# The head of the first expert's list in three pieces, and six more half chunks as split products whose low halves VectorE makes

## The chip, the core and the metric

The kernel runs on one core of a Trainium2 chip. Its time is the device time of one execution in microseconds (us). The engines work side by side, each on its own queue of instructions in order: TensorE (PE in the profile) multiplies, VectorE (DVE) and ScalarE (ACT) work on elements, GpSimd (POOL) issues gathers, scatters and accumulating transfers, SyncE (SP) issues most of the loads. Semaphores tie the queues together.

## The reference

Two parts follow each other. The first is an attention over channels: batch 4, 5056 positions, 256 channels.

```
qn = q / (norm(q, axis=1) + 1e-06);  kn = k / (norm(k, axis=1) + 1e-06)
s = kn.transpose(0, 2, 1) @ qn / tau          # 256 x 256 per batch
a = softmax(s, axis=-1)
x = v @ a                                     # 5056 x 256 per batch
```

The second is a mixture of eight experts over the 20224 rows of x. All 161792 logits are sorted; in that order each row goes to the first expert that still has room, with room for 2528 rows in each.

```
logits = x @ w_gate                           # 20224 x 8
for idx in argsort(-logits.flatten()):
    tok, e = idx // 8, idx % 8
    if assigned[tok] >= 0 or counts[e] >= 2528: continue
    assigned[tok] = e; counts[e] += 1
out[mask_e] = relu(x[mask_e] @ w1[e]) @ w2[e] # 256 -> 1024 -> 256
```

All of it is fp32, and the lists must come out as the sort makes them.

## The kernel before, in words

**Stages.** The scores k'q of the four batches come first, up to about 190 us, with the values of batch 0 among them. From 190 to 219 us stand the last softmax, the gates (a times w_gate) and the last logits. From 219 to 314 us stand the *turns*: the values of batches 1 to 3 that are still missing, and beside them the search for the first expert's list. Then the eight experts follow, layer 1 (line 1502) and layer 2 (line 1549), with the rows of each gathered from x_d in DRAM; the lists of the later experts are searched for beside these.

**Chunks and half chunks.** The 5056 rows of a batch are five chunks of eight tiles of 128 rows (the last is shorter). A half chunk is four tiles. Its x rows need eight products of 256 columns into two PSUM banks, which ScalarE empties (lines 271 and 587) and stores (line 277).

**Two kinds of products.** A plain half chunk (F in `TURNS`) multiplies in fp32 (line 267). A split one (C, "cloven") writes v and a as sums of a high part in the fp32r format and a low part, and adds three fp32r products: high by high, high by low, low by high (line 583). `PLAIN` and `CLOVEN` say which chunks are which: 16 half chunks F, of which 12 stand in the turns and four behind them, and 10 C. The split of v is `cleave`: ScalarE writes the negated v into the low tile (line 568), an accumulating transfer that GpSimd issues adds v once the copy is rounded, and ScalarE copies the high part (line 571). a of batch 2 is split by lines 550, 554 and 555 (`halve_a`). `PLACES` gives the tiles into which half chunks are split, and `BEHIND` the turn before which a tile is not free.

**The search.** The head of a list takes the largest logit of each row and its expert, and turns it into an integer key: two halves of 16 bits, `hi` and `klo`, and the expert's one-hot row `oh` (lines 611 to 660, 160 columns of 128 rows). The threshold is then found in eight rounds. In each, VectorE compares the keys with 15 thresholds (`ge`, line 730, in two halves), TensorE counts (20 products into one bank, line 695), VectorE takes sums of the counts (`Dm`, `Dr`, `Ex`, lines 698 to 704), TensorE totals them (line 708), and VectorE finds the hit and the next thresholds (`mxs`, `hit`, `thr`, lines 715 to 751). The lists are made from the threshold, and the rows gathered.

**Order.** From the turns on the program is written by a planner `o`. `o.tick` counts TensorE's time; a stream of steps (`yield ve(...)`, `yield "P", ...`) is given its place between the products by due times worked out from assumed costs, `o.post` places a single job, `FIRST_LAT` says from when VectorE is taken to be free for the first list. Each engine then works through its queue in that order.

Of the kernel before, what the change touches and what calls it, by code (L numbers as in the profile page):

```python
# [107 lines left out]
def attention_moe(ctx: ExitStack, tc: tile.TileContext, q, k, vt, tau, wg, w1t, w2t, tabs, out):  # L108
# [497 lines left out]

    def largest(to, x, tmp, n):
        while n > 1:
            h = n // 2
            yield ve(h * COLS)  # L610
            V.tensor_tensor(to[:, None] if n == 2 else tmp[:, 0:h], x[:, 0:h], x[:, n - h:n], op=OP.max)
            if n % 2:
                yield ve(COLS)
                V.tensor_tensor(to if n == 3 else tmp[:, 0], tmp[:, 0], x[:, h], op=OP.max)
            x, n = tmp, h

    def route(p, R):
# [10 lines left out]
        else:  # L628
            m = rtile("m")
            eq = rtile("eq", (128, E, COLS), BF)  # L630
            yield from largest(m, L, eq.bitcast(F32).rearrange("p r c -> p (r c)").rearrange("p (r c) -> p r c", c=COLS), R)
            key = rtile("t1").bitcast(I32)
            yield ve(COLS, 2)
            V.tensor_scalar(key.bitcast(F32), m, 0.0, None, op0=OP.add)
            flip = rtile("tie").bitcast(I32)
            yield ve(COLS, 2)
            V.tensor_scalar(flip, key, 31, 0x7fffffff, op0=OP.arith_shift_right, op1=OP.bitwise_and)
            yield ve(COLS)
            V.tensor_tensor(key, key, flip, op=OP.bitwise_xor)
            khi = rtile("khi", dt=I32)  # L640
            yield ve(COLS, 2)
            V.tensor_scalar(khi, key, -65536, None, op0=OP.bitwise_and)
            hi = rtile("hi", dt=I16)
            yield ve(COLS, 2)
            V.tensor_scalar(hi, khi, 1.0 / 65536.0, None, op0=OP.mult)
            klo = rtile("klo", dt=I32)
            yield ve(COLS, 2)
            V.tensor_scalar(klo, key, 0xffff, None, op0=OP.bitwise_and)
            yield ve(R * COLS)
            V.tensor_tensor(eq[:, 0:R], L[:, 0:R], m[:, None, :].to_broadcast([128, R, COLS]), op=OP.is_equal)  # L650
            yield ve(R * COLS)
            V.tensor_tensor(eq[:, 0:R], eq[:, 0:R], code9[:, 0:R, None].to_broadcast([128, R, COLS]), op=OP.mult)
            f = rtile("f")
            yield from largest(f, eq, eq, R)
# [1167 lines left out]
```

## Time and profile before

| what | us |
|---|---|
| median of three runs | 1213.45 |
| lowest and highest of them | 1211.61, 1217.76 |
| the profiled execution | 1215.57 |
| its span (first to last instruction) | 1213.8 |
| start of the turns in it | 219.13 |
| first product of layer 1 in it | 314.47 |

The profile is of one execution, and all rows below are of it. The span leaves out what lies around the first and the last instruction. A row of the timeline gives the start, the duration, the engine, the line, the operation, the tiles written and read, and in brackets how long the engine was idle before and what ended it. A product in fp32 has two records.

### The profile page before, as it was taken

What the parts mean: (1) busy time and instruction counts of PE and PEld (TensorE: products, weight loads), DVE (VectorE), ACT (ScalarE), POOL (GpSimd) and SP (SyncE); (2) the same over time, 40 slices, a digit from 0 to 9 for tenths busy, and PEclk for the clock granted to TensorE, in tenths of its full rate; (3) what the DMA queues carried; (4) which work ended last, traced back from release to release, by engine and by line L of the source; (5) the groups of instructions that cost most, each with busy time, mean ns of one, the idle gap of its engine ahead of it and who ended that gap; (6) DMA issues with size and microseconds to landing.
All of it is one profiled execution on the core that took longest, in us unless ns stands there. A gap on an engine that the chain in (4) does not pass through costs nothing.

```text
span 1213.8 us, 21117 instructions
## 1 busy us (share of the span) xinstructions
PE 1188.6 (98%) x7569; PEld 1044.0 (86%) x7569; DVE 891.1 (73%) x2493; ACT 597.7 (49%) x1314; POOL 453.1 (37%) x691
## 2 busy tenths in 40 slices
PE   7999999999999999999999999999999999999997
PEld 6889977898888888888888889888988898898997
DVE  6788695778788888988878788798786565555441
ACT  5667644655344444444454454464355644344331
POOL 1000001111353664555554554464444445444422
PEclk9999999999999999999999999999999999999999
DMA  8999996885335324534643454353234233433311
GB/s 304 356 397 318 409 321 213 181 235 218 108 101 151 88 72 128 167 92 116 172 127 88 107 165 140 100 156 121 86 124 145 86 119 124 145 94 99 108 61 35
DMA packets 76025, 193.50 MB, mean 159 GB/s; under 512 B 11792, under 2 KB 35600, under 8 KB 71312
## 3 DMA queue, kind: packets, MB, share of 16 engines
q0 software_dynamic: 26864, 74.08, 23.0%
q1 hardware_dynamic: 39088, 96.49, 22.8%
q10 hardware_dynamic: 9968, 21.59, 4.7%
q8 instruction: 59, 0.97, 0.3%
q14 instruction: 46, 0.38, 0.1%
HBM read 122.51 MB, written 58.98 MB: 150 GB/s over the span
## 4 chain that ended last, share of the span: by engine, by line
PE 80%; DVE 7%; issue 5%; DMA 3%; POOL 2%; ACT 2%; another core or an unknown queue 0%; SPq 0%; POOLq 0%; DVEq 0%; ACTq 0%
PE ph L1502 29%; PE py L1549 28%; PE s L345 8%; PE px L267 5%; PE pc L695 2%; PE px L308 2%; PE px L583 2%; DMA ua<-in_q_dram 2%; PE px L461 1%; POOL out_dram L1559 1%; DVE hL L1511 1%; DMA via<-xs 1%; DVE ua L1269 1%; PE pi L935 1%; DVE acc_k L355 1%
## 5 line engine op out<-in xcount | busy, mean ns | idle before, releaser
L1549 PE MATMUL py<-ua,hH 128*128 128x512 f32 (+2 forms) x1288 | 422.9, 382 | 0.0
L1502 PE MATMUL ph<-xH,ua 128*128 128x512 f32 (+1 forms) x1280 | 391.8, 380 | 0.8 <-DVE hL L1511 0.6
L1549 PE MATMUL py<-ua,hL 128*128 128x256 f32 (+1 forms) x1280 | 326.9, 275 | 0.0
L1506 ACT ACTIVATE hH<-ph 128x512 fp32r<-128x512 f32 (+1 forms) x320 | 189.3, 592 | 198.8 <-PE ph L1502 171.6
L1502 PEld LDWEIGHTS ph<-xH,ua 128*128 128x128 f32 x1280 | 241.1, 189 | 32.8 <-DVE hL L1511 4.2
L1511 DVE SCALAR_TENSOR_TENSOR hL<-ph,hH 128x512 fp32r<-128x512 f32 (+1 forms) x320 | 216.3, 677 | 62.4 <-ACT hH L1506 46.3
L1549 PEld LDWEIGHTS py<-ua,hH 128*128 128x128 f32 (+1 forms) x1288 | 233.0, 188 | 25.8
L1549 PEld LDWEIGHTS py<-ua,hL 128*128 128x128 f32 (+1 forms) x1280 | 242.4, 190 | 8.2
L1559 POOL DMA_INDIRECT out_dram<-y,idx x160 | 167.1, 1045 | 205.8 <-DVE y L1590 118.0
L1502 PE MATMUL ph<-xL,ua 128*128 128x512 f32 (+1 forms) x640 | 242.8, 379 | 0.7 <-DVE hL L1511 0.7
L1288 POOL DMA_INDIRECT xg<-x_d,src x160 | 163.7, 1023 | 80.1 <-issue 46.2
L345 PE MATMUL s<-ua 128*128 128x256 f32 (+1 forms) x640 | 144.0, 384 | 7.1 <-DMA ua<-in_q_dram 7.1
L345 PEld LDWEIGHTS s<-ua 128*128 128x128 f32 (+1 forms) x640 | 121.2, 192 | 26.5 <-DMA ua<-in_q_dram 7.5
L1502 PEld LDWEIGHTS ph<-xL,ua 128*128 128x128 f32 x640 | 121.0, 189 | 15.2 <-DVE hL L1511 1.1
L1570 ACT ACTIVATE y<-py 128x512 f32<-128x512 f32 x80 | 47.8, 597 | 114.9 <-PE py L1549 84.1
L1590 DVE TENSOR_TENSOR y<-py,y 128x256 f32<-128x256 f32 x79 | 33.5, 423 | 94.5 <-ACT y L1586 91.6
L354 ACT ACTIVATE sq<-ua 128x1024 f32<-128x1024 f32 (+1 forms) x80 | 76.6, 971 | 49.9 <-DMA ua<-in_k_dram 18.9
L1586 ACT ACTIVATE y<-py 128x256 f32<-128x256 f32 x80 | 30.6, 383 | 124.3 <-PE py L1549 106.4
L1299 POOL COPY spacer<-hH 1x1 f32<-1x1 f32 x102 | 26.7, 262 | 123.5 <-ACT hH L1506 120.2
L375 POOL TENSOR_SCALAR ny<-ny 128x4 f32<-128x4 f32 x4 | 2.0, 504 | 180.7 <-ACT ny L374 180.7
L1575 POOL DMA_DIRECT2D y<-y x36 | 35.6, 990 | 80.2 <-ACT y L1570 68.7
L1387 DVE TENSOR_TENSOR xL<-xT,xH 128x256 fp32r<-128x256 f32 x132 | 51.7, 432 | 9.6 <-ACT xH L1383 9.3
(346 smaller groups left out, 1577.7 us busy)
## 6 DMA issues: line engine op xcount, KB each, us to landing
x_d<-xs ACTq DMA_DIRECT2D x40, 512.0 KB
ua<-in_k_dram SPq DMA_DIRECT2D x35, 512.0 KB
ua<-in_q_dram SPq DMA_DIRECT2D x35, 512.0 KB
via<-xs SPq DMA_DIRECT2D x33, 512.0 KB
xT<-via SPq DMA_DIRECT2D x132, 128.0 KB
vr<-in_vt_dram SPq DMA_DIRECT2D x14, 1024.0 KB
y<-y POOLq DMA_DIRECT2D x36, 256.0 KB
ua<-in_vt_dram SPq DMA_DIRECT2D x4, 1024.0 KB
```

The lines of the kernel that those rows point to most:

```text
L267: mm = PE.matmul(px[:, i * C:i * C + width], lhsT=vs[b, c][:, kb, t + i, :], rhs=a_f[b][:, kb, 0:width], start=(kb == 0), stop=(kb == 1))
L345: newest[0] = PE.matmul(sb[:, ib * C:(ib + 1) * C], lhsT=kt[:np_, t, ib * 128:(ib + 1) * 128], rhs=qt[:np_, t, :], start=(first and t == 0 ...
L354: S.activation(sq[:n, t0:t1], t_[:n, t0:t1], AF.Square)
L1288: P.indirect_dma_start(out=xg[:n, i, :], out_offset=None, in_=rows, in_offset=bass.IndirectOffsetOnAxis(ap=routed[p]["src", col][:n, col:c ...
L1387: V.tensor_tensor(lo[:, a], rows[:, a], hi[:, a].bitcast(F32), op=OP.subtract)
L1502: PE.matmul(ph[:, 0:nt], lhsT=l[:, w], rhs=in_turn(x_, kb, nt).rearrange("p a m -> p m a"), start=(i == 0), stop=(i == 5))
L1506: S.activation(hH[:, fb, 0:nt], ph[:, 0:nt], AF.Relu)
L1511: V.scalar_tensor_tensor(hL[:, fb, 0:nt], ph[:, 0:nt], 0.0, hH[:, fb, 0:nt].bitcast(F32), op0=OP.max, op1=OP.subtract)
L1549: PE.matmul(to, lhsT=l[:, fb, tk], rhs=r, start=(fb == 0 and k_ == 0), stop=(fb == 7 and at_end), skip_group_check=twice)
L1559: sd = P.indirect_dma_start(out=out, out_offset=bass.IndirectOffsetOnAxis(ap=routed[p]["idx", col][:n, col:col + 1], axis=0), in_=y[:n], i ...
L1570: S.activation(y2[:n, :, i % 2], py[:n].rearrange("p (z m) -> p z m", z=2), AF.Copy)
L1575: P.dma_start(out=y2[:, 0], in_=y2[:, 1], accum_op=OP.add)
```

## The change

Three things are changed together.

1. **The head in three pieces.** `keys_of` makes the keys of a range of columns (`KNOWN`). Columns 0 to 79, whose logits are there early, are done around the last lengths and norms: twelve steps ahead of them, the rest behind the diagonal matrix. The fourth and fifth jobs of logits (columns 80 to 111) are moved ahead of the second half of chunk (1,1), their keys stand behind the softmax. Columns 112 to 159 stay in the first list's stream.
2. **Six more split half chunks.** Batch 1's (1,2), (1,3) and (1,4) go from `PLAIN` to `CLOVEN`: 10 F of which six stand in the turns, and 16 C. a of batch 1 is split too (`halve_a_1`, lines 643 to 649), with its low part by VectorE.
3. **Their low halves by VectorE.** The six (`BY_DVE`) have no negated copy and no transfer; ScalarE copies the high part (line 672) and VectorE subtracts it from v (line 676, 128x1024), placed by `o.post`. The other ten are made as before. A pool `own` of one tile, on the space of the closed stage of the scores, takes three of the half chunks. `first_w` (the first expert's weights) waits for twelve, the weights' splits for all sixteen split half chunks to be past.

```diff
-        "tail": [("w", (1, 1)), ("l", 3), ("l", 4), ("l", 5), ("l", 6), ("l", 7)]}
+        "tail": [("w", (1, 1)), ("l", 5), ("l", 6), ("l", 7)]}
 GATES_AT = (3, 3)
-FIRST_LAT = 3000
+FIRST_LAT = 2000
+KNOWN = (0, 80, 112)
+BEFORE_NORMS = 12
 HOMES = {(1, 0): "ub", (1, 1): "ub", (2, 4): "ua", (3, 0): "ua", (3, 1): "ua", (3, 2): "ua", (3, 3): "late", (3, 4): "late"}
-PLAIN = ((3, 0), (1, 2), (3, 1), (3, 2), (1, 3), (1, 4), (3, 3), (3, 4))
-CLOVEN = ((2, 4), (2, 0), (2, 1), (2, 2), (2, 3))
-TURNS = "FFCFCFCFCFCFCFCFCFFCFC"
-PLACES = ("ub0", "ub1", "ua0", "ua1", "ub0", "ub1", "vr", "ua0", "ua1", "ua2")
-BEHIND = {3: "FF", 4: "C", 5: "CC", 6: "FFFF", 7: "CCC", 8: "CCCC", 9: "FFFFFF"}
-FREED = (9, 10)
+PLAIN = ((3, 0), (3, 1), (3, 2), (3, 3), (3, 4))
+CLOVEN = ((2, 4, 0), (1, 2, 0), (2, 4, 4), (2, 0, 0), (1, 2, 4), (2, 0, 4), (2, 1, 0), (1, 3, 0), (2, 1, 4), (2, 2, 0), (1, 3, 4),
+          (2, 2, 4), (2, 3, 0), (1, 4, 0), (2, 3, 4), (1, 4, 4))
+BY_DVE = (1, 4, 7, 10, 13, 15)
+TURNS = "FFCCFCCCCFCCCCFCCCFCCC"
+PLACES = ("ub0", "ub1", "own", "ua0", "ua1", "ub0", "ub1", "own", "ua0", "ua1", "vr", "ub0", "own", "ua0", "vr", "ua1")
+AFTER = {4: (2, 0), 5: (0, 1), 6: (0, 2), 7: (0, 3), 8: (0, 4), 9: (0, 5), 11: (0, 6), 12: (0, 8), 13: (0, 9), 15: (0, 10)}
+FREED = 16
+CUT_LAT = 3000
...
+    def keys_of(tiles, R, a, b, scratch):
+        khi, hi, klo, f, oh = tiles
+        w = b - a
+        cols = slice(a, b)
+        m, key, flip, eq = scratch
+        Lc = L[:, 0:R, cols]
+        yield from largest(m, Lc, eq.bitcast(F32).rearrange("p r c -> p (r c)").rearrange("p (r c) -> p r c", c=w), R, w)
...
+        Q = R + R % 2
+        yield ve(Q * w)
+        V.tensor_tensor(oh[:, cols, 0:Q], f[:, cols, None].to_broadcast([128, w, Q]),
+                        code9[:, None, 0:Q].to_broadcast([128, w, Q]), op=OP.is_equal)
...
-                V.tensor_scalar(dq[:, jb], ident, rn[:, 2 + jb:3 + jb], None, op0=OP.mult)
+                cur["diag"] = V.tensor_scalar(dq[:, jb], ident, rn[:, 2 + jb:3 + jb], None, op0=OP.mult)
...
-                V.tensor_scalar(ac[:, ib, 0:C], u[:, ib], sm[:, ib:ib + 1], None, op0=OP.mult)
+                cur["soft"] = V.tensor_scalar(ac[:, ib, 0:C], u[:, ib], sm[:, ib:ib + 1], None, op0=OP.mult)
...
-            lt = wk.tile([128, 512], F32, name="turned").rearrange("p (b e) -> p b e", e=32)
+            if s < 3:
+                lt = wk.tile([128, 512], F32, name="turned")
+            else:
+                lt = wk.tile([128, TH, C], F32, name="sq", bufs=2).rearrange("p t c -> p (t c)")[:, 0:512]
...
+        def known(a, b):
+            w = b - a
+            y = wk.tile([128, TH, C], F32, name="sq", bufs=2).rearrange("p t c -> p (t c)")
+            scratch = [y[:, 0:w], y[:, w:2 * w].bitcast(I32), y[:, 2 * w:3 * w].bitcast(I32),
+                       y[:, 3 * w:7 * w].bitcast(BF).rearrange("p (r c) -> p r c", r=E)]
+            return keys_of(head_of["tiles"], E, a, b, scratch)
+
+        head_of["tiles"] = keyed()
         fill = halves((1, 0))
         next(fill)
         next(fill)
         aT = late(turned_a, cur["ac"])
         old = cur["ac"]
+        gen = known(KNOWN[0], KNOWN[1])
+        for _ in range(BEFORE_NORMS):
+            next(gen)
         cur["ac"] = late(softmax, sb, rn)
+        with tc.issue_after(cur["diag"].ins):
+            for _ in gen:
+                pass
         next(fill)
         late(gates, B - 2, old, aT)
         next(fill)
+        with tc.issue_after(cur["soft"].ins):
+            for n in (3, 4):
+                logits(n)
+            for _ in known(KNOWN[1], KNOWN[2]):
+                pass
         gates(B - 1, cur["ac"], turned_a(cur["ac"]))
...
+    def halve_a_1():
+        a = a_f[1][:, :, 0:C].rearrange("p k (m a) -> p k m a", a=2)
+        h = apart(apool.tile([128, 2, GW], F32R, name="a0"))[:, :, :, 0:128]
+        S.activation(h.rearrange("p a k m -> p k m a"), a, AF.Copy)
+
+        def low():
+            less = x_rows()[:, 0:2].rearrange("p k (m a) -> p k m a", a=2)
+            V.tensor_tensor(less, a, h.rearrange("p a k m -> p k m a").bitcast(F32), op=OP.subtract)
+            lo = apart(apool.tile([128, 2, GW], F32R, name="a1"))[:, :, :, 0:128]
+            S.activation(lo.rearrange("p a k m -> p k m a"), less, AF.Copy)
+            a_two[1] = [h, lo]
+        unit[0] += 1
+        o.post(o.pe + CUT_LAT, 600, low, unit[0])
+
+    cctx = ExitStack()
+    own = cctx.enter_context(tc.tile_pool(name="own", bufs=1))
     v_cut = []
+    lows_of = {}
 
     def cleave():
-        b, c, h = cloven[len(v_cut)]
-        home = PLACES[len(v_cut)]
-        y = (vp.tile([128, 2048], F32, name="vr", bufs=BUFS_V) if home == "vr" else
+        k_ = len(v_cut)
+        b, c, h = CLOVEN[k_]
+        home = PLACES[k_]
+        y = (own.tile([128, 2048], F32, name="own") if home == "own" else
+             vp.tile([128, 2048], F32, name="vr", bufs=BUFS_V) if home == "vr" else
              ffw.tile([128, 2048], F32, name=home)).bitcast(F32R)
         y = y.rearrange("p (z k n) -> p z k n", z=2, k=2)
         raw = vs[b, c][:, :, h:h + TH].rearrange("p k t n -> p k (t n)")
-        S.activation(y[:, 1], raw, AF.Copy, scale=-1.0)
-        P.dma_start(out=y[:, 1], in_=vt[b, c].rearrange("p (k n) -> p k n", k=2)[:, :, h * 128:(h + TH) * 128],
-                    accum_op=OP.add)
+        if k_ not in BY_DVE:
+            S.activation(y[:, 1], raw, AF.Copy, scale=-1.0)
+            P.dma_start(out=y[:, 1], in_=vt[b, c].rearrange("p (k n) -> p k n", k=2)[:, :, h * 128:(h + TH) * 128],
+                        accum_op=OP.add)
         S.activation(y[:, 0], raw, AF.Copy)
+        if k_ in BY_DVE:
+            unit[0] += 1
+            o.post(o.pe + CUT_LAT, 1150,
+                   lambda: V.tensor_tensor(y[:, 1], raw, y[:, 0].bitcast(F32), op=OP.subtract), unit[0])
+        lows_of[k_] = unit[0]
         v_cut.append(y.rearrange("p z k (t n) -> p z k t n", t=TH))
 
     def x_tiles_cut(k, t, xs, tick):
-        b = cloven[k][0]
+        b = CLOVEN[k][0]
+        if b == 1:
+            o.flush(lows_of[k])
         px = next_px()
...
+            if p == 0:
+                tiles, a = head_of["tiles"], KNOWN[-1]
+                scratch = [x[:, 0:COLS - a] for x in (m, key, flip)]
+                scratch.append(eq.rearrange("p r c -> p (r c)")[:, 0:E * (COLS - a)].rearrange("p (r c) -> p r c", r=E))
+            else:
+                tiles, a, scratch = keyed(), 0, (m, key, flip, eq)
+            yield from keys_of(tiles, R, a, COLS, scratch)
+            khi, hi, klo, f, oh = tiles
...
         def first_w():
+            assert past.count("C") >= 12
...
-            if cut_w[0] and o.pe > cut_w[0][0] and len(cut_w[0]) > 1 and past.count("C") >= FREED[cut_w[0][1][0]]:
+            if cut_w[0] and o.pe > cut_w[0][0] and len(cut_w[0]) > 1 and past.count("C") >= FREED:
...
         place = halve_a(2)
+        halve_a_1()
...
         for kind in TURNS:
-            while len(v_cut) < len(cloven) and len(v_cut) <= len(past) + 1:
-                want_ = BEHIND.get(len(v_cut), "")
-                if any(past.count(x) < want_.count(x) for x in set(want_)):
+            while len(v_cut) < len(CLOVEN) and len(v_cut) <= len(past) + 2:
+                f_, c_ = AFTER.get(len(v_cut), (0, 0))
+                if past.count("F") < f_ or past.count("C") < c_:
                     break
                 cleave()
...
         actx.close()
+        cctx.close()
```

The body of `keys_of` is the head that stood in `route`, with `Lc`, the range's columns, in place of all.

**VectorE, the first round of the first search.** `ge` is the compare, `oh` the last step of the head, `ua_1906` a low half (its numbers only tell tiles apart). Before:

```order
L660 TENSOR_TENSOR oh<-f,code_121 128x1280
L665 TENSOR_SCALAR eq<-ne_149 128x8
L686 TENSOR_SCALAR Ex<-ne_149 32x128
L730 TENSOR_TENSOR ge<-hi,th_134 128x10x120 x2
L698 TENSOR_TENSOR Dm<-pc,dmask 128x64
L701 TENSOR_REDUCE Dr<-Dm 128x8
L704 TENSOR_TENSOR Ex<-Dr,jsel 120x128
L715 TENSOR_REDUCE mxs<-pc 128x15
```

After:

```order
L272 TENSOR_TENSOR oh<-f,code_121 128x384
L738 TENSOR_SCALAR eq<-ne_149 128x8
L759 TENSOR_SCALAR Ex<-ne_149 32x128
L803 TENSOR_TENSOR ge<-hi,th_134 128x10x120 x2
L676 TENSOR_TENSOR ua_1906<-vr,ua_1906 128x1024
L771 TENSOR_TENSOR Dm<-pc,dmask 128x64
L774 TENSOR_REDUCE Dr<-Dm 128x8
L777 TENSOR_TENSOR Ex<-Dr,jsel 120x128
L788 TENSOR_REDUCE mxs<-pc 128x15
```

The head's last step has 384 elements in place of 1280, and a subtraction of 128x1024 stands between the compare and `Dm`.

**ScalarE, from the first copies of the turns to the high half that this subtraction reads.** Lines 568 and 571 before are 669 (negated) and 672 after; 271 is 329; `own` is the new tile. Before:

```order
L568 ACTIVATE ua_1800<-vr 128x1024
L571 ACTIVATE ua_1800<-vr 128x1024
L554 ACTIVATE a_two<-a_176 128x512
L555 ACTIVATE a_two<-xs 128x512
L271 ACTIVATE xs<-px 128x512 x2
L277 DMA x_d<-xs 128x1024
L271 ACTIVATE xs<-px 128x512 x2
L277 DMA x_d<-xs 128x1024
L568 ACTIVATE ua_1850<-vr 128x1024
L571 ACTIVATE ua_1850<-vr 128x1024
```

After:

```order
L669 ACTIVATE own<-ua_1569 128x1024
L672 ACTIVATE own<-ua_1569 128x1024
L636 ACTIVATE a_two<-a_179 128x512
L637 ACTIVATE a_two<-xs 128x512
L329 ACTIVATE xs<-px 128x512
L649 ACTIVATE a_1871<-xs 128x2x128x2
L329 ACTIVATE xs<-px 128x512
L335 DMA x_d<-xs 128x1024
L669 ACTIVATE ua_1878<-vr 128x1024
L672 ACTIVATE ua_1878<-vr 128x1024
L329 ACTIVATE xs<-px 128x512 x2
L335 DMA x_d<-xs 128x1024
L672 ACTIVATE ua_1906<-vr 128x1024
```

The third tile is now `own`, a third copy of a's halves (L649) stands between the first two evacuations, the fourth tile stands one pair of evacuations earlier, and behind the second store comes the single copy of `ua_1906`, without a negated one.

**VectorE, the eighth round.** Lines 730, 698, 701, 704 and 715 before are 803, 771, 774, 777 and 788 after; `ua_2532` and `ua_2582` are low halves. Before:

```order
L730 TENSOR_TENSOR ge<-low,thr 128x10x120 x2
L675 SCALAR_TENSOR_TENSOR eq<-hit,eq 128x120
L679 TENSOR_REDUCE eq<-eq 128x8
L681 TENSOR_REDUCE eq<-eq 128x8
L698 TENSOR_TENSOR Dm<-pc,dmask 128x64
L701 TENSOR_REDUCE Dr<-Dm 128x8
L704 TENSOR_TENSOR Ex<-Dr,jsel 120x128
L715 TENSOR_REDUCE mxs<-pc 128x15
```

After:

```order
L803 TENSOR_TENSOR ge<-low,thr 128x10x120
L676 TENSOR_TENSOR ua_2532<-vr,ua_2532 128x1024
L803 TENSOR_TENSOR ge<-low,thr 128x10x120
L748 SCALAR_TENSOR_TENSOR eq<-hit,eq 128x120
L752 TENSOR_REDUCE eq<-eq 128x8
L754 TENSOR_REDUCE eq<-eq 128x8
L676 TENSOR_TENSOR ua_2582<-vr,ua_2582 128x1024
L771 TENSOR_TENSOR Dm<-pc,dmask 128x64
L774 TENSOR_REDUCE Dr<-Dm 128x8
L777 TENSOR_TENSOR Ex<-Dr,jsel 120x128
L788 TENSOR_REDUCE mxs<-pc 128x15
```

One subtraction stands between the halves of the compare, and one ahead of `Dm`.

## Rows read from the trace of the kernel before

**Rows 1.** The page, sections 1 (busy us, share, count) and 4 (the chain).

```profile
PE 1188.6 (98%) x7569; PEld 1044.0 (86%) x7569; DVE 891.1 (73%) x2493; ACT 597.7 (49%) x1314; POOL 453.1 (37%) x691
...
PE 80%; DVE 7%; issue 5%; DMA 3%; POOL 2%; ACT 2%; another core or an unknown queue 0%; SPq 0%; POOLq 0%; DVEq 0%; ACTq 0%
```

**Rows 2.** Windows of the turns: range, us; busy us (count) by engine; clock; DMA.

```profile
219.10:280.00 60.90, 60.90 (x518) 56.41 (x516) 48.93 (x162) 34.34 (x56) 8.91 (x9) 1.00 0.76 209
280.00:314.40 34.40, 31.84 (x206) 27.92 (x203) 29.54 (x109) 20.02 (x53) 6.01 (x5) 1.00 0.60 212
```

**Rows 3.** TensorE waits, 185 to 315 us: us in total, times, longest.

```profile
PE pt L1455 <- DMA xg<-x_d,src: 1.2, 1, 1.2
PE pc L915 <- DVE cb L909: 0.7, 1, 0.7
PE pi L935 <- ACT ext L956: 0.5, 1, 0.5
```

**Rows 4.** Timeline, TensorE, start of turns: start, us, line, operation, tiles, count.

```profile
219.13 7.17 PE L267 MATMUL px<-a_last,ua 128*128 128x256 f32 x32
225.95 3.03 PE L583 MATMUL px<-a_two,ub 128*128 128x256 f32 x24
228.82 3.62 PE L267 MATMUL px<-a,vr 128*128 128x256 f32 x16
232.08 1.47 PE L583 MATMUL px<-a_two,ub 128*128 128x256 f32 x10
233.39 0.76 PE L695 MATMUL pc<-oh,ge 128*128 128x64 bf16 x20
233.98 1.47 PE L583 MATMUL px<-a_two,ub 128*128 128x256 f32 x11
235.29 0.23 PE L708 MATMUL pc<-Ex,ones_q 128*128 128x128 f32 x1
```

**Rows 5.** Timeline, VectorE, 190 to 219 us, the three long idle times.

```profile
191.72 0.16 DVE L369 COPY nrm<-pc 128x4 f32<-128x4 f32 x1 [3.69 <-PE pc L366]
...
196.70 0.88 DVE L399 SCALAR_TENSOR_TENSOR z<-s,rn,yy 128x256 f32<-128x256 f32 x2 [2.15 <-ACT yy L395]
...
213.61 0.72 DVE L464 STREAM_TRANSPOSE turned<-px 128x512 f32<-128x512 f32 x1 [5.12 <-PE pm L438]
```

**Rows 6.** Timeline, VectorE, head of the list and its first round.

```profile
220.37 0.82 DVE L611 TENSOR_TENSOR eq<-L 128x640 f32<-128x640 f32 x1
221.23 0.49 DVE L611 TENSOR_TENSOR eq<-eq 128x320 f32<-128x320 f32 x1
...
222.11 0.24 DVE L634 TENSOR_SCALAR t<-m 128x160 f32<-128x160 f32 x1
...
230.09 1.48 DVE L730 TENSOR_TENSOR ge<-hi,th 128x1200 bf16<-128x1200 int16 x2
234.19 0.23 DVE L698 TENSOR_TENSOR Dm<-pc,dmask 128x64 f32<-128x64 f32 x1 [2.62 <-PE pc L695]
```

**Rows 7.** Timeline, VectorE, an addition of 128x1024, in the scores.

```profile
180.81 1.22 DVE L355 TENSOR_TENSOR acc_k<-acc_k,sq 128x1024 f32<-128x1024 f32 x1
```

**Rows 8.** Timeline, ScalarE, copies of half chunks and evacuations.

```profile
215.38 1.06 ACT L568 ACTIVATE ua<-vr 128x1024 fp32r<-128x1024 f32 x1 [0.97 <-PE px L461]
216.34 1.04 ACT L571 ACTIVATE ua<-vr 128x1024 fp32r<-128x1024 f32 x1
...
227.34 1.06 ACT L568 ACTIVATE ua<-vr 128x1024 fp32r<-128x1024 f32 x1 [0.40 <-ACT xs L271]
...
229.25 1.07 ACT L587 ACTIVATE xs<-px 128x512 f32<-128x512 f32 x2
```

**Rows 9.** Timeline, TensorE, end of the turns, first rows, layer 1.

```profile
297.45 4.05 PE L267 MATMUL px<-a_last,vr 128*128 128x256 f32 x18
...
309.45 0.59 PE L1455 MATMUL pt<-identr,xg 128*128 128x128 f32 x2 [1.24 <-DMA xg<-x_d,src]
...
314.47 0.43 PE L1502 MATMUL ph<-xH,ua 128*128 128x512 f32 x1
```

**Rows 10.** TensorE waits in the experts, 314 to 1214 us.

```profile
PE pc L708 <- DVE Ex L704: 3.9, 6, 1.0
```

More of the change, by code (lines that the diff above doesn't have):

```diff
@@ L217, in attention_moe, with ve, largest @@
     V.memset(ne2[:, 1], 0.0)
+    hd = ctx.enter_context(tc.tile_pool(name="hd", bufs=1))
+    def ve(n, rate=1, psum=False, ptr=0):
+        return "V", ((120 if psum else 58) + n / rate) / 0.96 + 66 * ptr
+    def largest(to, x, tmp, n, w):
+        while n > 1:
+            h = n // 2
+            yield ve(h * w)
+            V.tensor_tensor(to[:, None] if n == 2 else tmp[:, 0:h], x[:, 0:h], x[:, n - h:n], op=OP.max)
+            if n % 2:
+                yield ve(w)
+                V.tensor_tensor(to if n == 3 else tmp[:, 0], tmp[:, 0], x[:, h], op=OP.max)
+            x, n = tmp, h
@@ new lines, in keyed @@
+    def keyed():
+        return [hd.tile(shape, dt, name=name) for name, shape, dt in (
+            ("khi", [128, COLS], I32), ("hi", [128, COLS], I16), ("klo", [128, COLS], I32), ("f", [128, COLS], F32),
+            ("oh", [128, COLS, E], BF))]
+    def keys_of(tiles, R, a, b, scratch):
[5 more added lines that the diff above has]
+        yield from largest(m, Lc, eq.bitcast(F32).rearrange("p r c -> p (r c)").rearrange("p (r c) -> p r c", c=w), R, w)
+        yield ve(w, 2)
+        V.tensor_scalar(key.bitcast(F32), m, 0.0, None, op0=OP.add)
+        yield ve(w, 2)
+        V.tensor_scalar(flip, key, 31, 0x7fffffff, op0=OP.arith_shift_right, op1=OP.bitwise_and)
+        yield ve(w)
+        V.tensor_tensor(key, key, flip, op=OP.bitwise_xor)
+        yield ve(w, 2)
+        V.tensor_scalar(khi[:, cols], key, -65536, None, op0=OP.bitwise_and)
+        yield ve(w, 2)
+        V.tensor_scalar(hi[:, cols], khi[:, cols], 1.0 / 65536.0, None, op0=OP.mult)
+        yield ve(w, 2)
+        V.tensor_scalar(klo[:, cols], key, 0xffff, None, op0=OP.bitwise_and)
+        yield ve(R * w)
+        V.tensor_tensor(eq[:, 0:R], Lc, m[:, None, :].to_broadcast([128, R, w]), op=OP.is_equal)
+        yield ve(R * w)
+        V.tensor_tensor(eq[:, 0:R], eq[:, 0:R], code9[:, 0:R, None].to_broadcast([128, R, w]), op=OP.mult)
+        yield from largest(f[:, cols], eq, eq, R, w)
+        yield ve(w)
+        V.tensor_tensor(f[:, cols], f[:, cols], U01[:, cols], op=OP.mult)
+        Q = R + R % 2
+        yield ve(Q * w)
+        V.tensor_tensor(oh[:, cols, 0:Q], f[:, cols, None].to_broadcast([128, w, Q]),
+                        code9[:, None, 0:Q].to_broadcast([128, w, Q]), op=OP.is_equal)
@@ L219, in attention_moe @@
+    head_of = {}
     ffw = ctx.enter_context(tc.tile_pool(name="ffw", bufs=1))
@@ L282, in attention_moe @@
         newest = [None]
+        cur = {}
         v_two = {}
@@ L501, in load_consts @@
             nc.scalar.dma_start(U01, tabs[:, 2])
-        cur = {}
         for b in range(B):
@@ L556, in halve_a @@
         return place
-    cloven = [(b, c, h) for b, c in CLOVEN for h in range(0, T, TH)]
+    def halve_a_1():
[12 more added lines that the diff above has]
+    own = cctx.enter_context(tc.tile_pool(name="own", bufs=1))
     v_cut = []
+    lows_of = {}
     def cleave():
-        b, c, h = cloven[len(v_cut)]
-        home = PLACES[len(v_cut)]
-        y = (vp.tile([128, 2048], F32, name="vr", bufs=BUFS_V) if home == "vr" else
+        k_ = len(v_cut)
[3 more added lines that the diff above has]
+             vp.tile([128, 2048], F32, name="vr", bufs=BUFS_V) if home == "vr" else
              ffw.tile([128, 2048], F32, name=home)).bitcast(F32R)
@@ L605, in attention_moe @@
     done = {}
[L607 to L615, printed above, removed]
     def route(p, R):
@@ L628, in route @@
         else:
-            m = rtile("m")
+            m, key, flip = rtile("m"), rtile("t1").bitcast(I32), rtile("tie").bitcast(I32)
             eq = rtile("eq", (128, E, COLS), BF)
[L631 to L654, printed above, removed]
@@ L1650, in attention_moe @@
                 k = past.count("C")
-                b, c, h = cloven[k]
+                b, c, h = CLOVEN[k]
                 xs = x_rows()
```

9 lines of the change are left out of this document (1 added, 8 removed).

## The prediction

> **What bounds the kernel now.** I read the page first, then the windows of the stage that the change touches, TensorE's waits there, and last its timeline beside those of VectorE and ScalarE. On the page the reader is to see that TensorE is busy for 1188.6 of 1213.8 us, and that the chain that ended last runs through it for 80% [rows 1]. So an edit is worth what it takes from TensorE's work or from its few waits. The stage of the change is 219 to 314 us, where the remaining half chunks of x = v a are multiplied while the first list is searched for. Up to 280 us TensorE is busy in all of it, 60.90 of 60.90 us, and after that in 31.84 of 34.40; the granted clock is 1.00, the 2.4 GHz level [rows 2]. TensorE's named waits there are three: 1.2 us for the first gathered rows, 0.7 for a VectorE copy, 0.5 for a ScalarE copy of the list [rows 3]. VectorE is busy 48.93 of the 60.90 us. The searching is therefore already beside the products, and hurrying it is worth only what its waits cost; but VectorE's results gate the counting products in TensorE's queue, and a late one stops everything behind it.
>
> **Part 1: six half chunks by three products.** Two half chunks of plain fp32 take from 219.13 to 225.95, 6.82 us, so 3.41 each (16 records, two to a product, so 0.43 a product of 256 columns). The next 24 products of a split half chunk and 16 records of a plain one end at 232.08: 6.13 us, so a split one takes 6.13 − 3.41 = 2.72 (0.113 a product) [rows 4]. Six times 3.41 − 2.72 = 0.69 is −4.14. A half chunk of each kind stands between these starts, so the price holds where they alternate; where split ones follow each other, which happens only now, 2.86 was the worst that I could work out from stretches with counting products between. Then the six save −3.3. I take −4.14.
>
> The Trainium skill, FP8 and Floating Point Precision, section TensorE Precision Notes, says that true FP32 makes four passes through the array, one for each pair of high and low halves. By it three products would be 0.75 of four, 2.56 instead of 3.41, and the six would save 5.1, a sum lower by 1.0. The rows show 2.72/3.41 = 0.80, so part of the saving is lost at each product; the rows decide.
>
> **Part 2: waits that go.** The list's first 0.5 [rows 3] was TensorE's block waiting for the ScalarE copy; in the new order it has split products to do ahead of that block, so the copy is done first: −0.5 (or nothing). The 0.7 stays. The rows of the first gather come at 309.45, which is 12.0 after the last split half chunk's end at 297.45, and between stand two plain chunks, transposes of the rest and the 1.24 of waiting [rows 4, 9]. Some 0.3 more of TensorE's work now stands between, so 0.95 is left: −0.3 (0 to −1.24). Together −0.8.
>
> **Part 3: the head of the list.** Before, the head begins behind the last logits at 220.37 and its first compare at 230.09 [rows 6]. From 640 to 320 elements an operation of two fp32 inputs falls from 0.82 to 0.49, so 0.155 + 0.00103 a column; the scalar operation of 160 is 0.24. By these the twelve steps on columns 0 to 79 that now precede the last lengths are 3.9 us, and the other five 1.85; VectorE has 3.69 idle before the lengths and 2.15 before the softmax's product [rows 5]. The 32 columns behind the softmax are 3.8, under 5.12 idle [rows 5]. What sticks out is at most 0.2. For the last 48 columns 4.8 is left of 9.7; two low halves (below) stand with them, 0.68 and 1.22, so the first compare starts at about 227.2 and is done at 228.7. TensorE reaches its first count 9.9 after the turns start (6.82 + 2.72 + three products), at 229.3: covered by 0.5.
>
> For this the logits of the list's fourth and fifth sixteen columns stand ahead of (1,1)'s last half, in TensorE's order, and between the last transposes of a and the gates only one product is left, where nine products of logits stood. The copy of the turned matrix between them takes 0.6 on ScalarE, and TensorE has that one product of 0.43 beside it. I take +0.3 (0 to 1.5, the top if the two banks that the logits hold until VectorE has turned them, behind the softmax, also stop (1,1)).
>
> **Part 4: new waits.** Six low halves are now VectorE subtractions of 128x1024. The page has no such subtraction; the nearest is an addition of that shape, 1.22 [rows 7]. Each waits for ScalarE's high copy (0.96 from start to start, 0.53 for a 512 evacuation, 0.40 for a store's issue, [rows 8]). Where it stands in the search's chain, everything of a round is queued behind: Dm, Dr and Ex, for which the totals product waits, and TensorE's products behind that.
> - Round 1: a low half stands between the compare and Dm. ScalarE's way to its high copy, from 220.5, where VectorE has copied the last logits (the head starts behind them at 220.37 now, [rows 6]): a whole new tile 1.92, the two copies of a 1.07, two evacuations with the halves of the other a 1.6, a store 0.40, a whole tile 1.92, two evacuations 1.07, a store 0.40, the copy 1.06: 9.5, done at 230.0. The low is done at 231.25; from Dm to the totals are 1.10 (234.19 to 235.29) [rows 4, 6], so 232.35. TensorE is there at 219.35 + 6.82 + 2.72 + 0.34 + 0.59 for the count + 1.36 for twelve products = 231.2. **+1.1** (0 to 1.6).
> - Round 5: a low stands ahead of the compare. From the third split half chunk's end ScalarE's queue, the low and the compare need 13.4; TensorE has 12.5 and 0.3 of wait: three split half chunks 8.16, two counts 1.18, two totals 0.14, seven plain products 3.0. **+0.6** (0 to 1.2).
> - Round 8: again ahead of Dm. 6.6 of ScalarE behind the half chunk before it, 1.22 and 1.10 are 8.9; TensorE has 24 products, the totals, eight plain products, the count and eight products, 7.7. **+1.15** (0 to 1.6).
> - Two others are covered, 3.97 against 3.81 and 4.27 against 3.8 by the same prices, within 0.5; the last is in the head.
>
> **Part 5: the rest.** One counting round of the second list (0.59 + 0.07) falls behind the start of the experts: moved, 0. The experts' planner fills other gaps in its other order. TensorE waits there six times for Ex, 3.9 us in all [rows 10]; I take 0, with ±1.5, since half of those waits would be a large change.
>
> Sum: −4.14 − 0.8 + 0.3 + 1.1 + 0.6 + 1.15 = −1.8, with 2.85 of new waits in it. Against the profiled span of 1213.8 this is 1212.0. The profiled execution took 1215.57, 1.77 more than its span and 2.12 more than the median of 1213.45, so I apply the change to the median: **1211.7**. Its own range, by the bounds above, is 1209.5 to 1213.5.
>
> **The rivals.**
> A, the low halves are hidden: ScalarE reaches its copies early, since it is busy for only 34.34 of 60.90 us [rows 2], and the three rounds do not wait. Against it: its queue is in order, and the copies stand behind evacuations that wait for TensorE. 2.85 less: 1208.8.
> B, slower: ScalarE becomes the bound between the third and the tenth split half chunk. There it has 18 evacuations of 0.535, nine stores of 0.40, fourteen half copies of 0.955 and six short copies, 27.7 us, against 28.5 of TensorE's. For it: a copy's record is 1.06 while its start-to-start is 0.96 [rows 8]. If each of 45 instructions costs 0.08 more, ScalarE needs 31.3 and TensorE waits 2.8 for its banks, and the lows come later by as much once more in the last round, 1.6: 1211.7 + 4.4 = 1216.1. It decides from the point at which the queue exceeds 28.5. Against it: the present share of ScalarE.
> C, nothing is left: the split half chunks cost 2.86 one behind the other (+0.8), and the experts' other order takes 1 us more (+1): 1213.5. For it: [rows 10] hold 3.9 us of waits that an order can move. Against it: nothing in the rows says in which direction.
>
> **How the numbers follow.** The forecast has 0.45, A 0.25, B 0.15, C 0.15. About 0.5%, 6.1 us, is what a measurement of this kernel can tell from no change: faster means under 1207.4, slower over 1219.5. All four cases lie between. A with a cheaper split product or experts' order could reach under 1207.4: 0.10. B with both ends at their worst reaches over 1219.5: 0.06. The range goes from A's lower part, 1207.5, to B's, 1216.
>
> **What would show it.** In the profile after: sixteen split half chunks of 2.7 us, TensorE's waits for Ex or for the low half of about 1 us in rounds 1 and 8, a first compare near 227 us, no new wait between 190 and 219 above 1 us, and the first product of layer 1 at about 312.3 instead of 314.47 [rows 9]. Wrong would be: waits for ScalarE's evacuations in the turns above 2 us, a start of layer 1 later than 314, or experts that take more than 2 us longer or shorter than the 899.3 from 314.47 to the span's end.

## The result, and the profile after

The changed kernel is slower by some 0.7%: median 1220.29 us of nine executions (1216.98 to 1225.27), before 1213.38 of nine; the ratio is 1.0066, interval 1.0047 to 1.0085. The profiled execution took 1216.98 (span 1215.2). It is the quickest of the nine, so its trace shows less than the whole loss, and e1 below took a second one.

The page of after, sections 1 and 4, answers to [rows 1]:

```profile
PE 1185.2 (98%) x7617; PEld 1043.1 (86%) x7617; DVE 902.9 (74%) x2532; ACT 606.3 (50%) x1322; POOL 449.0 (37%) x689
...
PE 69%; DVE 13%; DMA 6%; issue 6%; ACT 3%; POOL 2%; ACTq 0%; SPq 0%; POOLq 0%; DVEq 0%
```

TensorE has 3.4 us less to do, and the span is 1.4 longer: 4.8 us more of it is idle, and VectorE has 13% of the last chain where it had 7%. The waits of TensorE, first from 185 to 315 us (for [rows 3]), then in the experts (for [rows 10]):

```profile
PE pc L781 <- DVE Ex L777: 1.9, 2, 1.0
PE pt L1528 <- DMA xg<-x_d,src: 1.8, 1, 1.8
PE pc L988 <- DVE cb L982: 1.1, 1, 1.1
PE pc L768 <- DVE ge L803: 0.4, 2, 0.2
...
PE ph L1575 <- ACT xH L1456: 2.8, 1, 2.8
PE pc L781 <- DVE Ex L777: 2.7, 2, 1.7
```

The turns begin at 220.26 and layer 1 at 313.75 (219.13 and 314.47 in [rows 4, 9]): 93.49 us instead of 95.34, so 1.85 were gained there, 0.66 of it by a counting round that now stands behind layer 1's start. From layer 1 to the end are 901.45 instead of 899.33: 2.1 were lost in the experts (0.66 of it that counting round), and 10 in e1's execution (909.5).

**The turns did what was forecast.** VectorE's timeline of round 1, then TensorE's at the totals of rounds 1 and 8 and at the first rows:

```profile
228.36 1.48 DVE L803 TENSOR_TENSOR ge<-hi,th 128x1200 bf16<-128x1200 int16 x2
231.44 1.22 DVE L676 TENSOR_TENSOR ua<-vr,ua 128x1024 fp32r<-128x1024 f32 x1 [1.60 <-ACT ua L672]
232.59 0.22 DVE L771 TENSOR_TENSOR Dm<-pc,dmask 128x64 f32<-128x64 f32 x1
```

```profile
233.48 0.33 PE L781 MATMUL pc<-Ex,ones_q 128*128 128x128 f32 x1 [1.01 <-DVE Ex L777]
...
274.78 0.33 PE L781 MATMUL pc<-Ex,ones_q 128*128 128x128 f32 x1 [0.88 <-DVE Ex L777]
...
309.93 0.28 PE L1528 MATMUL pt<-identr,xg 128*128 128x128 f32 x1 [1.85 <-DMA xg<-x_d,src]
```

The low half in round 1 waits 1.60 for ScalarE's copy and takes 1.22, and TensorE's totals come 1.01 late; in round 8 they come 0.88 late. In round 5 the count waits 0.43 for the compare, in two parts.

**What was not forecast** stands near 430 us, at the first layer 1 of the second expert. ScalarE's timeline, GpSimd's, TensorE's, and windows of TensorE (range; length, busy and count; granted clock, DMA share, GB/s):

```profile
427.21 0.80 ACT L1456 ACTIVATE xH<-xT 128x256 fp32r<-128x256 f32 x2 [1.29 <-DMA xT<-via]
433.17 0.60 ACT L1643 ACTIVATE y<-py 128x512 f32<-128x512 f32 x1 [5.16 <-DMA out_dram<-y,idx]
433.66 0.74 ACT L1456 ACTIVATE xH<-xT 128x256 fp32r<-128x256 f32 x2
```

```profile
428.26 1.10 POOL L1632 DMA_INDIRECT out_dram<-y,idx  x1 [3.49 <-DMA y<-y]
429.35 0.09 POOL L1631 MEMSET spacer<- 1x1 f32 x1
429.67 1.00 POOL L1632 DMA_INDIRECT out_dram<-y,idx  x1 [0.23 <-issue]
```

```profile
434.46 0.48 PE L1575 MATMUL ph<-xH,ua 128*128 128x512 f32 x1 [2.82 <-ACT xH L1456]
```

```profile
434.00:436.00 2.00, 0.96 (x2) 1.00 0.02 6
436.00:438.00 2.00, 1.63 (x4) 0.51 0.36 129
438.00:440.00 2.00, 2.00 (x10) 0.64 0.86 114
440.00:442.00 2.00, 2.00 (x11) 1.00 0.01 1
```

The rows of this chunk now come by transfer through DRAM (`via`, `xT`) and are split by ScalarE in two halves. Before, TensorE transposed them. ScalarE and TensorE of the kernel before, at the same place:

```profile
427.30 0.59 ACT L1458 ACTIVATE xH<-pt 128x512 fp32r<-128x512 f32 x1
430.44 0.60 ACT L1570 ACTIVATE y<-py 128x512 f32<-128x512 f32 x1 [2.55 <-PE py L1549]
```

```profile
432.88 0.38 PE L1502 MATMUL ph<-xH,ua 128*128 128x512 f32 x1
```

There the second half is split at 427.30, ahead of the next copy of y, which waits for TensorE alone, and layer 1 begins without a wait. In the changed kernel the order is another. Between the halves a copy of y (line 1643) waits 5.16 us for its buffer, which a scatter is still reading; ScalarE's queue is in order, so the second half comes behind it, at 433.66, and TensorE stands for 2.82. Behind the pause its granted clock is 0.51 and 0.64 in the next two windows, for the most part the lower level of 1.2 GHz; that costs 2 × (0.49 + 0.36) = 1.7 us more.

It is a choice of the planner. It takes the transfer if the chunk's rows count as landed while more than 15.5 us of work lie before their layer 1. In the planner's own count of ns, it looks at 187154 in before, with 16128 left, and has the rows landed at 187387: too early by 232, before rounding. In the changed kernel the list is planned earlier, and at the same point of the order (16128 left) it looks at 182091, with the rows landed at 181475: the test holds. A second choice turns with it: the first rows of the fourth expert, which came by transfer before, are now transposed by TensorE. No wait of layer 1 stands there in the trace of after (653.73).

### The profile page after: what moved, and what is told of

Same layout as the page of the kernel before. It is cut to its first block, busy times and chain, and to the rows that moved or that the text cites. A ratio compares the mean times of both kernels' runs of the same rounds, so it can differ in the third digit from the quotient of the medians.

```text
span 1215.2 us, 21254 instructions
## 1 busy us (share of the span) xinstructions
PE 1185.2 (98%) x7617; PEld 1043.1 (86%) x7617; DVE 902.9 (74%) x2532; ACT 606.3 (50%) x1322; POOL 449.0 (37%) x689
## 4 chain that ended last, share of the span: by engine, by line
PE 69%; DVE 13%; DMA 6%; issue 6%; ACT 3%; POOL 2%; ACTq 0%; SPq 0%; POOLq 0%; DVEq 0%
PE ph L1575 29%; PE py L1622 26%; PE s L404 4%; DMA ua<-in_q_dram 3%; PE pc L768 2%; PE px L691 2%; PE px L325 2%; PE px L367 1%; POOL out_dram L1632 1%; DVE acc_q L414 1%; DMA x_d<-xs 1%; DVE acc_k L414 1%; DVE nf L471 1%; DVE hL L1584 1%; DMA via<-xs 1%
## 5 line engine op out<-in xcount | busy, mean ns | idle before, releaser
L1372 POOL COPY spacer<-hH 1x1 f32<-1x1 f32 x100 | 23.1, 231 | 113.2 <-ACT hH L1579 109.7
```

## The experiments

Each was run beside the kernel before. "Last rows" is the first product of the plain half chunks behind the last split one. Start, stretches and clock are of the profiled execution, in us:

| kernel | ratio, interval | turns from | to last rows | to layer 1 | to the end | clock |
|---|---|---|---|---|---|---|
| before | 1 | 219.13 | 78.32 | 17.02 | 899.3 | 0.999 |
| after | 1.0066, 1.0047 to 1.0085 | 220.26 | 76.69 | 16.80 | 901.5 | 0.997 |
| e1 | 1.0059, 1.0037 to 1.0081 | 220.70 | 76.68 | 16.63 | 909.5 | 0.995 |
| e2 | 0.9988, 0.9973 to 1.0003 | 227.51 | 76.67 | 18.36 | 898.0 | 0.995 |
| e3 | 1.0039, 1.0022 to 1.0057 | 220.54 | 78.31 | 17.29 | 904.6 | 0.995 |
| e4 | 1.0017, 1.0003 to 1.0031 | 222.80 | 76.68 | 16.75 | 901.1 | 0.998 |
| e5 | 1.0053, 1.0029 to 1.0076 | 224.14 | 75.17 | 21.28 | 899.8 | 0.993 |
| e6 | 0.9984, 0.9971 to 0.9998 | 220.88 | 78.57 | 16.00 | 894.6 | 0.999 |
| e7 | 1.0200, 1.0178 to 1.0222 | 217.85 | 72.15 | 24.42 | 916.1 | 0.991 |
| e8 | 1.0033, 1.0013 to 1.0052 | 218.91 | 78.30 | 17.03 | 903.6 | 0.996 |
| e9 | 0.9994, 0.9978 to 1.0009 | 222.20 | 78.56 | 16.03 | 897.1 | 0.997 |
| e10 | 0.9987, 0.9970 to 1.0005 | 218.68 | 75.89 | 18.63 | 897.8 | 0.997 |

**e1: the changed kernel again.** No edit.

> The changed kernel once more, for a second profile. Theory P (the experts' order gives it back: the first rows of the second expert now come by transfer, their split waits on ScalarE behind a copy that waits for a scatter, TensorE stops and its clock falls behind it): ratio 1.005 to 1.008 again, the first product of layer 1 again within 1 us of 313.75, and in the profile again one wait of layer 1 for ScalarE's split of 2.5 us or more near 430 us, with a granted clock under 0.95 in the 10 us behind it; the time beyond the first profile's 1215.2 span comes from such stretches. Theory T (the turns' new waits for VectorE's low halves are longer in most executions than in the first profile): layer 1 starts at 316 us or later.

TensorE's timeline and windows of e1:

```profile
435.90 0.48 PE L1575 MATMUL ph<-xH,ua 128*128 128x512 f32 x1 [3.30 <-ACT xH L1456]
```

```profile
438.00:440.00 2.00, 2.00 (x6) 0.50 0.64 131
440.00:442.00 2.00, 2.00 (x9) 0.50 0.41 49
442.00:444.00 2.00, 2.00 (x6) 0.50 0.00 0
```

Theory P's wait is there again, longer, and the clock stays at 0.50 twice as long (0.86 and 0.80 over the two 10 us from 430: 3.4 us lost). Layer 1 starts at 314.01: theory T falls.

**e2: the second expert's first rows by transposes.**

```diff
-BY_PE = ((0, 0), (0, 1), (0, 2))
+BY_PE = ((0, 0), (0, 1), (0, 2), (1, 0))
```

> The changed kernel with the first rows of the second expert turned by TensorE's transposes, as they were before the change; all of the turns is as in the changed kernel. Theory P: the wait near 430 us and the low clock behind it go, 5 to 8 us less than the changed kernel: ratio to the kernel before 0.997 to 1.001, about 1212. Theory T: nothing but 0 to 1 us changes, ratio 1.005 to 1.007, about 1220.

`BY_PE` lists the chunks that TensorE transposes whatever the planner's test says. 0.9988: the loss is gone by one entry that touches neither head nor half chunks. With it the planner also gives the fourth expert's first rows back to the transfer, so every chunk goes the way it went in the kernel before. Among e2's waits of TensorE there is none for ScalarE's split, and the clock from 430 to 440 is 1.00. The change without the planner's choice is about 1.5 us quicker than before, by a ratio whose interval just holds 1; the forecast for all of it was −1.75.

**e3 and e8: the kernel before, with the transfer.**

```diff
-landed.get(todo[0], 1e12) <= o.pe and
+landed.get(todo[0], 1e12) - 500 * (todo[0] == (1, 0)) <= o.pe and
```

> The kernel before with one planner number moved by 500 ns, so that the second expert's first rows come by transfer as in the changed kernel; its turns, its head and its half chunks are those of before. Theory P: a wait of layer 1 for ScalarE's split of 2 us or more and a fall of the clock appear, ratio 1.004 to 1.008, about 1219. Theory T: ratio 0.999 to 1.001.

> The kernel of e3 (before, with the second expert's first rows by transfer) once more, for a second profile, since in its first the long wait of layer 1 stood at 609 us and not near 430. If the transfer's place in the order makes the wait there: a wait of 2 us or more for ScalarE's split or its follower between 425 and 445 us this time. If what costs is any wait for rows that come by transfer, wherever a landing is late: none there, one of 2 us or more elsewhere. Ratio 1.002 to 1.006 in both; 0.999 to 1.001 if e3's 1.0039 was chance.

1.0039 and 1.0033, so the choice alone, with every other chunk as before, slows the kernel before as well. But the long wait stood elsewhere, in both profiles at layer 1 of the third expert's fourth chunk. In e8, in turn: TensorE, the transfer's issue on SyncE's queue, the weights' fetch on GpSimd's, and ScalarE:

```profile
432.33 0.48 PE L1502 MATMUL ph<-xH,ua 128*128 128x512 f32 x1 [0.86 <-ACT xH L1383]
607.40 0.80 PE L1502 MATMUL ph<-xH,ua 128*128 128x512 f32 x1 [3.08 <-ACT xH L1383]
```

```profile
594.65 1.73 SPq L1358 DMA_DIRECT2D xT<-via  x4
```

```profile
594.36 1.41 POOL L1250 DMA_INDIRECT ub<-in_w1t_dram,ei  x1 [0.30 <-issue]
596.08 0.94 POOL L1250 DMA_INDIRECT ub<-in_w2t_dram,ei  x1 [0.30 <-issue]
```

```profile
606.59 0.76 ACT L1383 ACTIVATE xH<-xT 128x256 fp32r<-128x256 f32 x2 [7.35 <-DMA xT<-via]
```

That chunk comes by transfer in the kernel before too, from whose trace these are the same three rows:

```profile
593.61 1.73 SPq L1358 DMA_DIRECT2D xT<-via  x4
```

```profile
594.96 1.43 POOL L1250 DMA_INDIRECT ub<-in_w1t_dram,ei  x1 [0.30 <-issue]
```

```profile
599.75 0.78 ACT L1383 ACTIVATE xH<-xT 128x256 fp32r<-128x256 f32 x2
```

There the transfer is issued 1.35 us ahead of the weights, and the split runs 6.1 after it; in e8 it is issued 0.3 behind the first of them, and the split runs 11.9 after it (e3: 0.2 and 12.3). The issue is later since the write to `via` ahead of it lands later (SyncE waits 4.1 for it, 2.4 before); why, was not traced. The second of e8's two expectations holds: no wait of 2 us near 430, one of 3.08 elsewhere. A late split of rows that come by transfer costs here too, but why the shifted order makes this one late is not shown.

**e4: both halves of the split ahead of the copy of y.**

```diff
-                split_x(*ch, ready[ch])
-                ready[ch] += 1
+                for _ in range(2 if ch == (1, 0) else 1):
+                    split_x(*ch, ready[ch])
+                    ready[ch] += 1
```

> The changed kernel, the second expert's first rows by transfer as there, but both halves split one behind the other on ScalarE, ahead of the copy of y that waits for a scatter (some later chunk is then planned another way too). Theory Q (ScalarE's queue: the second half's split stood behind that copy): the wait of layer 1 for that split falls from 2.8 or 3.3 us to under 0.7, no low clock at 430 to 450 us, ratio 0.997 to 1.002. Theory R (the transfer itself lands late, or the clock falls there for another reason): wait of 2 us or more again, ratio 1.004 to 1.007.

The 2.82 is gone with the transfer kept, and the clock from 430 to 450 is 1.00: theory Q. The ratio falls from 1.0066 and 1.0059 to 1.0017 though the fourth expert's first rows are still transposed, so that choice is not what cost most. One thing else differs: the second expert's third chunk is transposed here and came by transfer in the changed kernel. The copy of y waits as long (ScalarE, first fence); now layer 1's own copies stand behind it, for 1.29 (TensorE, second fence). A later wait for Ex is longer, 3.22 where after has 1.72, with 1.7 us of lower clock behind it, which after does not have there:

```profile
429.91 1.53 ACT L1456 ACTIVATE xH<-xT 128x256 fp32r<-128x256 f32 x4 [1.29 <-DMA xT<-via]
437.01 1.08 ACT L1644 ACTIVATE y<-py 128x512 f32<-128x512 f32 x2 [5.57 <-DMA out_dram<-y,idx]
```

```profile
439.36 0.48 PE L1576 MATMUL ph<-xH,ua 128*128 128x512 f32 x1 [1.29 <-DVE hL L1585]
723.03 0.30 PE L781 MATMUL pc<-Ex,ones_q 128*128 128x64 f32 x1 [3.22 <-DVE Ex L777]
```

**e5 and e10: low halves moved away from Dm.** With e2's edit; `LOW_LAT` gives, in ns, how far behind TensorE's place a low half is due (3000 for the others): e5 has `{4: 5000, 15: 6000}`, e10 `{4: 4500}`:

```diff
-            o.post(o.pe + CUT_LAT, 1150,
+            o.post(o.pe + LOW_LAT.get(k_, CUT_LAT), 1150,
```

> The changed kernel with the second expert's first rows by transposes, and the low halves of the fifth and the last VectorE half chunk placed later, so that none stands any more between a compare and Ex. By the terms of the sum (1.1, 0.6 and 1.15 forecast; 1.0, 0.4 and 0.9 in the profile) TensorE's waits for Ex in the turns go: layer 1 starts 1.5 to 2.5 us earlier than with e2, ratio to before 0.996 to 0.998. Against it: the lows stand elsewhere in the chain, and the list is no earlier: 0.998 to 1.000.

> As e2 (the changed kernel, second expert's first rows by transposes, the same chunks by transposes as before), with the low half of the fifth split half chunk alone placed later; the waits for Ex and ge in the first and fifth round, 1.4 us in e2, go, that of the eighth stays. If the products set the end of the turns: ratio 0.996 to 0.998. If the chain of last store, gather and first rows gives it back as it did in e5: 0.998 to 1.000, with a wait for the first rows longer than e2's 1.8.

The waits for Ex in the turns fall from 1.9 us (e2) to none (e5) and 0.4 (e10), but those for the compare rise from 0.4 to 0.8, and 0.5 for a ScalarE copy is new; so e10's expectation of the first and fifth round holds in part. The last rows come 1.5 (e5) and 0.8 us (e10) sooner than in e2. Little or nothing of it is left at layer 1: from the last rows to it are 21.28 (e5) and 18.63 (e10), where e2 has 18.36, and after and e1, whose clock does not fall there, 16.80 and 16.63. TensorE in e5, its first rows, and a window behind them:

```profile
311.88 0.28 PE L1528 MATMUL pt<-identr,xg 128*128 128x128 f32 x1 [1.37 <-DMA xg<-x_d,src]
312.48 0.28 PE L1528 MATMUL pt<-identr,xg 128*128 128x128 f32 x1 [0.32 <-DMA xg<-x_d,src]
313.89 0.37 PE L1528 MATMUL pt<-identr,xg 128*128 128x128 f32 x1 [1.14 <-DMA xg<-x_d,src]
```

```profile
314.00:320.00 6.00, 6.00 (x18) 0.51 0.02 6
```

The end of the turns is the chain from the last split half chunk's store through four gathers to the first rows, with products beside it; in e5 the pause there is followed by the lower clock (0.51 for 6 us: 2.9 lost). In e5 the planner also has one chunk each of the third and fourth expert transposed that came by transfer in e2, which makes its ratio no measure of the low halves alone. e10 keeps e2's choice of chunks, and its ratio is e2's.

**e6 and e9: the head alone.** The changed code with `PLAIN`, `CLOVEN`, `TURNS` and `PLACES` of before, `BY_DVE = ()`, no split of batch 1's a; e6 with e2's edit, e9 without it.

> The head in three pieces alone: the turns, half chunks and accumulating transfers of before, the second expert's first rows by transposes (left to itself the planner would choose the transfer here too). The search is off TensorE's path but for its last wait for the first rows: ratio 0.999 to 1.001, the first product of layer 1 within 0.7 us of before's when counted from the start of the turns. If the head carried the gain, 0.996 to 0.998.

> The head in three pieces alone, as in e6, but with the planner left free: it then takes the transfer for the second expert's first rows. Theory P: 3 to 8 us more than e6, so a ratio of 1.001 to 1.005, with a wait of layer 1 for a split or a landing of 2 us or more that e6 does not have. If the transfer costs only where the six half chunks are split too: as e6, 0.997 to 1.000.

0.9984: e6 has the lowest ratio, and the only interval against before that lies under 1; it overlaps those of e2, e9 and e10. In the turns it is 0.8 us shorter than before (94.57). Its first rows are waited for no more, since two counting rounds of the second list stand there now; the rest it gains in the experts, where two more chunks come by transfer than before (the second expert's second, the third's first). All three changes with the choice held (e2, 0.9988) are no quicker than the head alone: these runs show no gain of the six half chunks for the whole kernel. With the transfer (e9) there is a wait of 0.60 at that chunk, one of 0.94 at the next, which TensorE transposes in e9 and not in e6, and none of 2 us: both choices together cost 0.1%, within the intervals. So theory P in its simple form, that the transfer always costs 3 us or more, falls: it costs where the split lands behind a blocked copy or a late transfer.

**e7: the six half chunks alone**, head undivided (`KNOWN = (0,)`, the early pieces and moved logits taken out, `FIRST_LAT = 3000`), with e2's edit.

> The six more split half chunks alone, with the head undivided behind the last logits, the second expert's first rows by transposes. By the sum, the six save 4.1 us, and without the divided head TensorE waits longer in the first round, since two low halves stand in the head as well: turns 0 to 2.5 us shorter than before's 95.3, ratio 0.997 to 1.001. If the head is what makes room for the low halves: 1.001 or more.

1.02: the second case of the expectation, far above its 1.001. The last rows come after 72.15 us, so the products are quick; then TensorE waits for the rows of most chunks that it transposes. Its waits in the experts:

```profile
PE pt L1517 <- DMA xg<-x_d,src: 12.9, 6, 3.7
PE pc L757 <- DVE ge L792: 2.1, 3, 1.5
```

So without the divided head the six half chunks gain nothing: the turns take 96.57 us, 1.2 more than before, although the products are done 6.2 sooner. But in e7 two chunks of the fourth expert are transposed that came by transfer before, and why the lateness goes on into the fourth expert was not traced; so how much of the 1.02 is the missing head is not shown.

## Why the prediction was wrong

- **Part 1, six products saved**: right. Split half chunks one behind the other take 2.68 to 2.86 (276.78 to 279.46, 285.99 to 288.85), the price of 2.72 within them.
- **Part 2, waits that go**: half right. The 0.5 went; the wait for the first rows grew from 1.24 to 1.85 where 0.95 was forecast, as the rows came 13.0 us behind the last split half chunk, not 12.0. The 0.7 grew to 1.08.
- **Part 3, the head**: first compare at 228.36, that is 8.1 behind the start of the turns, as forecast (227.2, 8.1 behind 219.13). From the norms' products to the turns the tail is 0.4 longer; +0.3 was forecast. But after's trace is one of the kinder ones: the tail is 28.5 us in all four profiles with the undivided head (before, e3, e7, e8), and with the divided one 0.4 longer in after, 1.3 in e1, 0.8 in e2, 2.2 in e4, 1.8 in e5, 0.2 in e6 and e10, 0.8 in e9. The 3.69 us of idle time into which the twelve steps were put is VectorE's lead over TensorE in one execution. In e4 VectorE has no such lead; the steps, begun at 192.21, hold back the copy of the norms, and TensorE waits for the diagonal matrix:

```profile
192.21 0.47 DVE L233 TENSOR_TENSOR sq<-L 128x320 f32<-128x320 f32 x1
195.68 0.15 DVE L428 COPY nrm<-pc 128x4 f32<-128x4 f32 x1
```

```profile
198.45 0.68 PE L452 MATMUL pc<-nf,ones_f 128*128 128x128 f32 x4 [1.34 <-DVE nf L451]
```

- **Part 4, new waits**: 1.01, 0.43 and 0.88 for 1.1, 0.6 and 1.15; right.
- So in after's trace the turns and their tail come to −1.4 (−1.85 + 0.43), and without the round that only moved to −0.8, where −1.8 was forecast; the first rows' wait makes up 0.9 of the difference. With e1's longer tail the same count gives −0.1 (93.31 for the turns). For the whole kernel e2's ratio gives −1.5, with an interval from −3.3 to +0.4.
- **Part 5, the rest, failed**: "I take 0, with ±1.5". I saw that the planner fills the experts in another order, but bounded it by a move of waits that [rows 10] already held, about half of their 3.9 us. The stretch from layer 1 to the end grew by 2.1 in after's execution and by 10.2 in e1's. The order can also choose another way for a chunk's rows, with waits that before's trace doesn't show, and the pauses of 2.82 and 3.30 us there cost 1.7 and 3.4 more by the lower clock behind them. The table shows how far this term can move: with turns that differ by a few us, the stretch from layer 1 to the end lies between 894.6 and 916.1.
- Rival C had the place (the experts' order), priced at +1, and rival B the sign, at another place: ScalarE does become late, not between the third and the tenth half chunk, but near 430 us, 210 behind the start of the turns. TensorE had no named wait for ScalarE in the turns. (B's sum counts 45 instructions where its own list has 47; that is 0.2 us.)

What stays open: how much of the loss is the pause and how much the clock in a typical execution. In the two profiles it was 2.8 + 1.7 and 3.3 + 3.4 us, of a loss of some 8.6 us by the ratios (1.0059 less e2's 0.9988). And why the loss of e1's trace is 8 us larger than that of after, though its pause and its clock explain 2.2 of them and its other named waits in the experts another 2.

## What to carry to other kernels

Where a planner with thresholds writes the order, a change of one stage must be judged with the choices of the later stages listed before and after: one test that turned by 0.2 us here outweighed all that was computed with care. Hold such choices fixed (e2) to measure the edit itself, and choose again afterwards. And idle time of an engine in one trace is its lead in that execution: work that is put there is free only as long as the lead lasts (e4's 1.34). Work that the next matmul needs should not stand in an in-order queue behind a copy that waits for a buffer that a transfer is still reading.

## What the runs showed of the hardware

- Pauses of TensorE of 2.79 to 3.75 us in the experts were followed by the lower clock wherever they stood (after and e1 near 435, e3 and e8 near 608, e4 and e5 near 725, e7 near 440 and 648), in the first six at a cost of 1.7 to 3.4 us; one of 2.61 in e7 (424) was not. Pauses of 1.8 for the first rows were sometimes (e2, e10), sometimes not (after, e1, e4). The Trainium skill, TensorE: Matmul & The Clock Gate, section on the HAM clock gate, says that the clock is halved behind idleness and comes back with work; these rows agree with that, in the middle of a kernel in which TensorE is busy for 98% of the span.
- A transfer of 512 KB in four parts took at most 6.1 us from issue to its reader when issued 1.35 ahead of two weight fetches of 1 MB, and 11.9 when issued 0.3 behind the first. That the fetches are the cause is not shown, since no run moved the issue alone. The Trainium skill, DMA: Bandwidth & Descriptors, section Issuing engines are not separate DMA queues, says that transfers from SyncE, ScalarE and GpSimd share the same engines and interleave; the two traces fit that.
